# K weights, K products and phi passes divided at column 384 instead of 320

## The chip, the cores and the metric

The kernel runs on one core of one Trainium2 chip. The metric is the device time of one execution in microseconds (us), the median over several runs. The trace beside it is of one profiled execution of the same program; its times are counted from the start of its span. The engines are TensorE (PE in the profile, with its weight loads on a row of their own, PEld), VectorE (DVE), ScalarE (ACT), GpSimd (POOL) and SyncE (SP), which issues most of the DMAs.

## The reference, cut to what matters

Two blocks read the same x (one batch, S = 2048 rows, D = 640 columns), and their results are added to it: linear attention with 32 heads of 20 columns on the layer-normed x, and a small mixture-of-experts style block on the 8 rows with the highest score r.

```python
def _A_ref(x, wqkv, wo):
    qkv = (x @ wqkv).reshape(B, S, 3, H, Dh).transpose(2, 0, 3, 1, 4)
    q, k, v = qkv[0], qkv[1], qkv[2]
    phi = lambda t: jnp.where(t > 0, t + 1, jnp.exp(t)) + 1e-6
    pq, pk = phi(q), phi(k)
    kv = jnp.einsum("bhsd,bhse->bhde", pk, v)
    z = jnp.einsum("bhsd->bhd", pk)
    num = jnp.einsum("bhqd,bhde->bhqe", pq, kv)
    den = jnp.einsum("bhqd,bhd->bhq", pq, z)[..., None] + 1e-6
    return (num / den).transpose(0, 2, 1, 3).reshape(B, S, D) @ wo

def _B_ref(x, w_r, w_gate, w_up, w_down):
    r = x @ w_r
    idx = jnp.argsort(-r, axis=-1)[:, :8]
    x_sel = jnp.take_along_axis(x, idx_e, axis=1)
    y = (silu(x_sel @ w_gate) * (x_sel @ w_up)) @ w_down
    y = y * sigmoid(r at idx)
    return x + y scattered to the rows idx

x = A_x
xn = _layernorm(x)
return x + _A_ref(xn, A_wqkv, A_wo) + _B_ref(xn, B_w_r, B_w_gate, B_w_up, B_w_down)
```

The change touches the K part of `x @ wqkv`, `phi(k)`, and the score `r`, whose weights ride as one more column beside the K weights.

## The kernel before

The 2048 rows are T = 16 tiles of 128 rows. Everything is in bf16 with fp32 sums in PSUM, one tensor `PS` of 8 banks of 512 columns. The order of every engine's work is written out by hand: the calls in the source, from top to bottom, are the order on each engine's queue, and an engine that waits holds up all that stands behind it on that queue.

**First stage, by tile t.** DVE takes the statistics of a tile in two halves of 320 columns (`ln_a`, `ln_b`, lines 151 and 154; these halves stay), aggregates them (`ln_g`), ACT makes 1/sigma of it (`ln_r`, lines 160 and 161), and DVE writes the normed tile into `XX[:, t, 0]` (`ln_xn`, line 165). The transposed tile goes into `xnT`: for t < 4 by PE transposes (`tr_mm`, line 174) and copies out of PSUM (`tr_cp`, lines 181 and 183), from t = 4 on by a DMA transpose on SP's queue (`tr_dma`, line 186). Then `K(t)` (line 210) multiplies with the K weights, which lie in `wk` in two parts: `wkh[0]`, columns 0 to 319 of K, and `wkh[1]`, columns 320 to 639 with the weights of r as a 321st column behind them (written by ACT at line 135). Part h = 0 goes to PSUM bank b, part h = 1 to bank b + 1 (b is 6, for tile 1 it is 4), five matmuls each (KC = 5 row blocks of the weights). Part 1 is placed at column `off(t, 1)` = 15 - t, so that the r column of each tile stays behind in a column of bank 7 of its own; tile 1, in bank 5, is kept separately. From t = 5 on, one weight load of zeros (`pad`, line 249) goes ahead of each part, and two more stand between the matmuls of `G`.

ACT then makes Exp and Relu of each part (`PHe` line 226, `PHr` line 229, both parts in turn by `PHa`), into `ek` and `rk`, 640 columns wide, and DVE joins both parts at once in `PHb` (line 245: min(exp, 1) + relu) into `pk[:, t]`. `G(t)` (lines 254 and 261) sums the product of the normed tile and `pk` over all tiles in banks 0 to 5.

The first four tiles are interleaved by hand in small steps (`KA` is weight blocks 0 and 1, `KB` blocks 2 to 4). From t = 4 on one loop runs: PE has `K(t)` and then `G(t - 1)`; ACT has `PHa(t)`, the small `ln_r(t + 3)`, and for t > 12 a pass `xpx` (line 198, x + xn of one tile); DVE has `PHb(t - 1)`, `ln_xn(t + 2)` and statistics.

**Between the stages.** `corner` (line 275) adds the last block of G in bank 6. `rcopy` (lines 237 and 238) copies the scores out of bank 7, the last of them on DVE; after it `q_pe(0, 0, 7)` (line 482), the first group of the Q products, writes that bank. Then come `PHb(15)` and `G(15)`.

**The rest** (Q products and their phi, denominators, routing and the expert block, the merged output matrix, the output products at line 754) uses none of what is changed, except that `Mb` takes over the place of `wk` later on, at its own width. Its output pieces are also 320 wide, or 256 and 384 for the first four tiles.

**DMA issues at the start.** ACT's queue has the weights of r and then `wkh[0]`; SP's queue has x tiles 0 to 3, one each, then `wkh[1]`, then x in three loads of four tiles.

Of the kernel before, what the change touches and what calls it, by code (L numbers as in the profile page):

```python
# [7 lines left out]
P = 128  # L8
S = 2048
D = 640  # L10
# [3 lines left out]
T = S // P  # L14
KC = D // P
# [14 lines left out]
BF16 = mybir.dt.bfloat16  # L30
# [3 lines left out]
AF = mybir.ActivationFunctionType  # L34
# [4 lines left out]
def kernel(  # L39
# [13 lines left out]
    pe, dve, act, pool, sp = nc.tensor, nc.vector, nc.scalar, nc.gpsimd, nc.sync  # L53
# [3 lines left out]
    wqkv_v = A_wqkv.rearrange("(kc p) n -> p kc n", p=P)  # L57
# [7 lines left out]
    PS = psp.tile([P, 8, 512], F32, name="PS")  # L65

    def st(shape, dt, name, tag=None):
        return sb.tile(shape, dt, name=name, tag=tag or name)
# [5 lines left out]
    wk = st([P, KC, WS], BF16, "wk", "wkM")  # L74
# [16 lines left out]
    rbf = st([P, T], BF16, "rbf")  # L91
# [4 lines left out]
    MR = st([P, T], F32, "MR")  # L96

    HW = 320
    wkh = [wk[:, :, 0:HW], wk[:, :, HW + 64 :]]


    def ld(eng, dst, src):
        eng.dma_start(dst, src)
# [4 lines left out]
    dve.memset(MVf[:], 0.0)  # L108
    wr = st([KC, P], BF16, "wr")
    ld(act, wr[:], B_w_r.rearrange("(kc p) -> kc p", p=P))  # L110
    ld(act, wkh[0], wqkv_v[:, :, D : D + HW])
    ld(sp, XX[:, 1, 1, :], x_v[:, 1, :])
    ld(sp, XX[:, 2, 1, :], x_v[:, 2, :])
    ld(sp, XX[:, 3, 1, :], x_v[:, 3, :])
    ld(sp, wkh[1][:, :, 0:HW], wqkv_v[:, :, D + HW : 2 * D])
    for a, b in ((4, 8), (8, 12), (12, 16)):
        ld(sp, XX[:, a:b, 1, :], x_v[:, a:b, :])
    sp.dma_start_transpose(xnT[:, 0:4, S - P : S], zero[:])
# [1 line left out]
    def warm4(w):  # L120
        pe.matmul(PS[:, 7, 0:w], lhsT=nc.const_aps.tensor(0.0, (P, P), F32),
                  rhs=nc.const_aps.tensor(0.0, (P, w), F32), start=True, stop=True)
# [9 lines left out]
    warm4(256)  # L132
    pe.transpose(PS[:, 3, :].bitcast(BF16)[:, 0:KC], wr[:], ident[0:KC, 0:KC])
    warm4(512)
    act.copy(wkh[1][:, :, HW], PS[:, 3, :].bitcast(BF16)[:, 0:KC])
    kv1 = st([P, NG, GC], BF16, "kv1")
    kv2 = st([P, NG, GC], BF16, "kv2")
    xsT = st([P, KC, 32], BF16, "xsT")
# [62 lines left out]
    def off(t, h):  # L201
        return T - 1 - t if t != 1 and h else 0

    def K(t, hs=(0, 1), b=6, ks=range(KC)):
        for h in hs:
            if t > 4:
                pad(1)
            w = HW + h
            for kc in ks:
                pe.matmul(  # L210
                    PS[:, b + h, off(t, h) : off(t, h) + w],
                    lhsT=xnT[:, kc, t * P : (t + 1) * P],
                    rhs=wkh[h][:, kc, 0:w],
                    start=(kc == 0),
                    stop=(kc == KC - 1),
                )

    phis = {}

    def phi_src(t, h, b):  # L220
        return PS[:, b + h, off(t, h) : off(t, h) + HW]

    def PHe(t, h, b=6):
        if t not in phis:
            phis[t] = tuple(tmp.tile([P, D], BF16, tag=k, name=k, bufs=3) for k in ("ek", "rk"))
        act.activation(phis[t][0][:, h * HW : (h + 1) * HW], phi_src(t, h, b), AF.Exp)  # L226

    def PHr(t, h, b=6):
        act.activation(phis[t][1][:, h * HW : (h + 1) * HW], phi_src(t, h, b), AF.Relu)  # L229

    def PHa(t, hs=(0, 1), b=6):
        for h in hs:
            PHe(t, h, b)
            PHr(t, h, b)

    def rcopy():
        act.copy(rbf[:, 0 : T - 2], PS[:, 7, HW : HW + T - 2])
        dve.tensor_copy(rbf[:, T - 1 : T], PS[:, 7, HW + T - 1 : HW + T])

    def rcopy1(b):  # L240
        act.copy(rbf[:, T - 2 : T - 1], PS[:, b, HW : HW + 1])

    def PHb(t):
        ek, rk = phis[t]
# [2 lines left out]
    def pad(n):  # L247
        for _ in range(n):
            pe.ldweights(zero[:, 0:P])  # L249
# [106 lines left out]
    tr_mm(1, 0, 2)  # L356
    tr_cp(0, 1, 0, act)
    K(0, (0,), 6, KA)
    ln_b(2)
    tr_cp(1, 0, 2, act)  # L360
    tr_mm(1, 1, 2)
    ones(1)
    K(0, (0,), 6, KB)
    tr_cp(1, 1, 2, act)
    ln_g(2)
    ln_a(3)
    K(1, (0,), 4, KA)
    ln_r(2)
    ln_b(3)
    K(1, (0,), 4, KB)  # L370
    PHe(0, 0, 6)
    ln_xn(2)
    K(0, (1,), 6, KA)
    PHr(0, 0, 6)
    K(1, (1,), 4, KA)
    ln_g(3)
# [6 lines left out]
    ln_xn(3)  # L383
    K(1, (1,), 4, KB)
    PHe(0, 1, 6)
    tr_cp(2, 1, 0, dve)
    PHr(0, 1, 6)
    tr_mm(3, 0, 2)
    ln_a(4)
    K(2, (0,), 6, KA)  # L390
    rcopy1(5)
    PHe(1, 0, 4)
    tr_mm(3, 1, 2)
# [100 lines left out]
    for t in range(T - 1):  # L494
        corner(t)
    rcopy()
    q_pe(0, 0, 7)
    PHb(T - 1)
# [457 lines left out]
```

## Time and profile before

| | us |
|---|---|
| median of 3 runs | 106.52 (106.29 to 106.86) |
| the profiled execution's own time | 106.34 |
| its span | 104.6 |
| PE busy in it | 99.7 (95%), granted clock 1.0 throughout |
| DVE busy | 82.8 (79%) |
| ACT busy | 68.8 (66%) |
| the K products, line 210: matmuls | 160 |
| the phi passes, lines 226 and 229: busy | 14.1 and 14.0 |

In the profile's groups of instructions, a row is line, engine, operation, tile written and tiles read, shape, count, then busy time and the mean duration in ns of one. A matmul's duration is its latency, ends are modelled, and matmuls overlap: the rate is read from the chain of waits, where a row is start, time, and the instructions on the chain. In the timeline a row is start, time, engine, line, operation, and in brackets the idle time ahead of it with what ended it; several in a row of one kind are one row, which then shows the shape of the first.

### The profile page before, as it was taken

The page shows a single profiled execution, that of the slowest core. Times are in us where ns is not written, and L with a number is a line of the kernel's source. Part 1 is how long each engine was busy: PE and PEld are TensorE (multiplying, and loading weights), DVE is VectorE, ACT ScalarE, POOL GpSimd, SP SyncE. Part 2 cuts the span into 40 slices and gives each one's busy share as a digit, 9 for nine tenths or more (in the row PEclk, how much of TensorE's full clock was granted, in tenths as well). Part 3 has the DMA queues.
Part 4 walks back from the last instruction along what each step waited for, and adds up shares of the span by engine and source line. Part 5 has one row for each costly group of instructions (what it writes and reads, how often), then busy time and mean ns, then how long its engine had stood idle before and what let it go on. Part 6 is the DMA issues. An engine that isn't in the chain of part 4 may idle for free.

```text
span 104.6 us, 2773 instructions
## 1 busy us (share of the span) xinstructions
PE 99.7 (95%) x916; PEld 72.6 (69%) x1148; DVE 82.8 (79%) x187; ACT 68.8 (66%) x171; POOL 15.9 (15%) x60
## 2 busy tenths in 40 slices
PE   6889999999999999999999999999999999999980
PEld 3257666668888888888777777875567767777760
DVE  1797999988888897873787867878988997888870
ACT  4289957666666666888599999876993996000000
POOL 7800000520000000000000026370000500000140
PEclk9999999999999999999999999999999999999999
DMA  2999938334655555899998999911470136895344
GB/s 67 304 341 382 271 64 58 77 66 96 147 126 101 133 121 117 180 288 337 229 386 282 337 337 379 350 50 39 133 255 9 30 101 205 150 376 211 132 129 125
DMA packets 23024, 19.67 MB, mean 188 GB/s; under 512 B 10594, under 2 KB 21474, under 8 KB 23010
## 3 DMA queue, kind: packets, MB, share of 16 engines
q1 hardware_dynamic: 21880, 19.01, 63.2%
q10 hardware_dynamic: 842, 0.46, 1.6%
q8 instruction: 8, 0.13, 0.5%
q0 software_dynamic: 288, 0.01, 0.3%
q14 instruction: 6, 0.05, 0.1%
HBM read 13.80 MB, written 3.65 MB: 167 GB/s over the span
## 4 chain that ended last, share of the span: by engine, by line
PE 90%; DVE 3%; DMA 2%; issue 1%; DVEq 0%
PE PS L210 21%; PE PS L482 21%; PE PS L754 20%; PE PS L254 15%; PE PS L261 4%; DMA XX<-in_A_x_dram 2%; PE PS L706 2%; PE PS L666 1%; PE PS L548 1%; PE PS L174 1%; PE PS L730 1%; PE PS L677 1%; PE PS L275 1%; DVE stats L151 1%; DVE XX L165 1%
## 5 line engine op out<-in xcount | busy, mean ns | idle before, releaser
L210 PE MATMUL PS<-wk,xnT 128*128 128x320 bf16 (+1 forms) x160 | 25.4, 300 | 0.0
L254 PE MATMUL PS<-pk,XX 128*128 128x512 bf16 x75 | 22.7, 379 | 0.0
L482 PE MATMUL PS<-xnT,wq 128*128 128x512 bf16 x97 | 22.2, 379 | 0.2
L754 PE MATMUL PS<-Mb,pqT 128*128 128x320 bf16 (+4 forms) x165 | 22.1, 295 | 0.0
L249 PEld LDWEIGHTS <-zero 128*128 128x128 bf16 x224 | 18.2, 97 | 5.5
L226 ACT ACTIVATE ek<-PS 128x320 bf16<-128x320 f32 x32 | 14.1, 441 | 9.9 <-PE PS L210 9.9
L754 PEld LDWEIGHTS <-pqT 128*128 128x128 bf16 x165 | 15.8, 98 | 4.7 <-issue 0.3
L210 PEld LDWEIGHTS <-xnT 128*128 128x128 bf16 x160 | 15.2, 97 | 4.7 <-issue 0.2
L245 DVE SCALAR_TENSOR_TENSOR pk<-ek,rk 128x640 bf16<-128x640 bf16 x16 | 13.1, 819 | 4.8 <-ACT rk L229 4.5
L539 DVE SCALAR_TENSOR_TENSOR pqT<-qe,qr 128x512 bf16<-128x512 bf16 x20 | 13.5, 685 | 2.9 <-ACT qr L491 2.9
L490 ACT ACTIVATE qe<-PS 128x512 bf16<-128x512 f32 x20 | 12.3, 616 | 3.2 <-PE PS L482 3.2
L261 PE MATMUL PS<-pk,XX 128*128 128x128 bf16 x64 | 14.0, 219 | 0.3
L229 ACT ACTIVATE rk<-PS 128x320 bf16<-128x320 f32 x32 | 14.0, 438 | 0.0
L482 PEld LDWEIGHTS <-wq 128*128 128x128 bf16 x100 | 11.6, 118 | 2.9 <-issue 0.2
L491 ACT ACTIVATE qr<-PS 128x512 bf16<-128x512 f32 x20 | 12.3, 616 | 0.0
L763 DVE TENSOR_TENSOR o<-PS,XX 128x640 bf16<-128x640 f32 x11 | 9.0, 822 | 2.9 <-PE PS L754 2.0
L254 PEld LDWEIGHTS <-XX 128*128 128x128 bf16 x80 | 7.8, 98 | 4.5
L198 ACT ACTIVATE XX<-XX,MR,SR 128x640 bf16<-128x640 bf16 x11 | 9.4, 913 | 0.0
L151 DVE BATCH_NORM_STATS2 stats<-XX 128x6 f32<-128x320 bf16 x16 | 7.4, 461 | 1.9 <-DMA XX<-in_A_x_dram 1.9
L165 DVE TENSOR_SCALAR XX<-XX,MVf,SR 128x640 bf16<-128x640 bf16 (+2 forms) x17 | 7.2, 432 | 0.6 <-ACT SR L161 0.6
L154 DVE BATCH_NORM_STATS2 stats<-XX 128x6 f32<-128x320 bf16 x16 | 7.7, 480 | 0.0
L267 POOL MEMSET XX<- 128x1 bf16 x18 | 1.8, 102 | 35.7 <-DVE XX L165 20.2
(114 smaller groups left out, 100.0 us busy)
## 6 DMA issues: line engine op xcount, KB each, us to landing
out_dram<-o SPq DMA_DIRECT2D x15, 160.0 KB, 2.0
XX<-in_A_x_dram SPq DMA_DIRECT2D x3, 640.0 KB, 7.9
wg<-in_B_w_gate_dram SPq DMA_DIRECT2D x5, 384.0 KB, 8.6
wu<-in_B_w_up_dram SPq DMA_DIRECT2D x5, 384.0 KB, 6.1
wd<-in_B_w_down_dram SPq DMA_DIRECT2D x1, 1920.0 KB, 10.6
wv<-in_A_wqkv_dram SPq DMA_DIRECT2D x5, 160.0 KB, 3.1
wq<-in_A_wqkv_dram SPq DMA_DIRECT2D x1, 800.0 KB, 5.9
hi_d<-XX SPq DMA_DIRECT2D x1, 800.0 KB, 4.0
```

The costliest lines, as they stand in the source:

```text
L210: pe.matmul(PS[:, b + h, off(t, h) : off(t, h) + w], lhsT=xnT[:, kc, t * P : (t + 1) * P], rhs=wkh[h][:, kc, 0:w], start=(kc == 0), stop=( ...
L226: act.activation(phis[t][0][:, h * HW : (h + 1) * HW], phi_src(t, h, b), AF.Exp)
L229: act.activation(phis[t][1][:, h * HW : (h + 1) * HW], phi_src(t, h, b), AF.Relu)
L245: dve.scalar_tensor_tensor(out=pk[:, t, :], in0=ek[:], scalar=1.0, in1=rk[:], op0=ALU.min, op1=ALU.add)
L249: pe.ldweights(zero[:, 0:P])
L254: pe.matmul(PS[:, a, :], lhsT=lhsT, rhs=pk[:, t, 0:512], start=(t == 0), stop=(t == T - 1),)
L261: pe.matmul(PS[:, 5, a * P : (a + 1) * P], lhsT=lhsT, rhs=pk[:, t, 512:D], start=(t == 0 and a == 0), stop=(t == T - 1), skip_group_check= ...
L482: pe.matmul(PS[:, bank, :], lhsT=by5(wq[:, kc, :])[:, m, :], rhs=xnT[:, kc, tb * TBLK : (tb + 1) * TBLK], start=(kc == 0), stop=(kc == KC ...
L490: act.activation(e, PS[:, bank, :], AF.Exp)
L491: act.activation(r, PS[:, bank, :], AF.Relu)
L539: dve.scalar_tensor_tensor(out=pqT[:, m, tb * TBLK : (tb + 1) * TBLK], in0=e, scalar=1.0, in1=r, op0=ALU.min, op1=ALU.add,)
L754: pe.matmul(PS[:, b, o : o + c1 - c0], lhsT=pqT[:, kc, t * P : (t + 1) * P], rhs=Mb[:, kc, c0:c1], start=(kc == 0), stop=(kc == KC - 1))
```

## The change

The border between part 0 and part 1 of K moves from column 320 to column 384. Part 0 of the weights then has 384 columns, part 1 has 256 and the column for r, at place 256 of that part. The loads of both parts, the K products, the Exp and Relu passes and the places from which the scores are copied follow. No instruction is added, removed or moved on any engine: 80 matmuls go from 320 to 384 columns and 80 from 321 to 257; 32 ACT passes go from 320 to 384 columns and 32 to 256; the load on ACT's queue goes from 5 x 320 to 5 x 384 elements per partition, the one on SP's queue from 5 x 320 to 5 x 256. `PHb`, `G` and all else keep their shapes. All of `wk` is as wide as before, and part 1 still begins at column 384 of it.

```diff
     HW = 320
-    wkh = [wk[:, :, 0:HW], wk[:, :, HW + 64 :]]
+    KH = ((0, 3 * P), (3 * P, D))
+    W1 = D - 3 * P
+    wkh = [wk[:, :, 0 : 3 * P], wk[:, :, 3 * P :]]
...
-    ld(act, wkh[0], wqkv_v[:, :, D : D + HW])
+    ld(act, wkh[0], wqkv_v[:, :, D : D + KH[0][1]])
...
-    ld(sp, wkh[1][:, :, 0:HW], wqkv_v[:, :, D + HW : 2 * D])
+    ld(sp, wkh[1][:, :, 0:W1], wqkv_v[:, :, D + KH[1][0] : 2 * D])
...
-    act.copy(wkh[1][:, :, HW], PS[:, 3, :].bitcast(BF16)[:, 0:KC])
+    act.copy(wkh[1][:, :, W1], PS[:, 3, :].bitcast(BF16)[:, 0:KC])
...
     def K(t, hs=(0, 1), b=6, ks=range(KC)):
...
-            w = HW + h
+            w = KH[h][1] - KH[h][0] + h
...
     def phi_src(t, h, b):
-        return PS[:, b + h, off(t, h) : off(t, h) + HW]
+        return PS[:, b + h, off(t, h) : off(t, h) + KH[h][1] - KH[h][0]]
...
-        act.activation(phis[t][0][:, h * HW : (h + 1) * HW], phi_src(t, h, b), AF.Exp)
+        act.activation(phis[t][0][:, KH[h][0] : KH[h][1]], phi_src(t, h, b), AF.Exp)
...
-        act.activation(phis[t][1][:, h * HW : (h + 1) * HW], phi_src(t, h, b), AF.Relu)
+        act.activation(phis[t][1][:, KH[h][0] : KH[h][1]], phi_src(t, h, b), AF.Relu)
...
     def rcopy():
-        act.copy(rbf[:, 0 : T - 2], PS[:, 7, HW : HW + T - 2])
-        dve.tensor_copy(rbf[:, T - 1 : T], PS[:, 7, HW + T - 1 : HW + T])
+        act.copy(rbf[:, 0 : T - 2], PS[:, 7, W1 : W1 + T - 2])
+        dve.tensor_copy(rbf[:, T - 1 : T], PS[:, 7, W1 + T - 1 : W1 + T])
...
     def rcopy1(b):
-        act.copy(rbf[:, T - 2 : T - 1], PS[:, b, HW : HW + 1])
+        act.copy(rbf[:, T - 2 : T - 1], PS[:, b, W1 : W1 + 1])
```

## The prediction

> **What bounds the kernel now.** I read the page's chain of waits by engine first, then the chain in order of time, then the places in it where PE is not at its rate.
>
> ```profile
> PE 90%; DVE 3%; DMA 2%; issue 1%; DVEq 0%
> 6.97 1.15 PE PS L210 x8
> 8.12 0.03 issue
> 8.15 0.71 PE PS L210 x4
> ...
> 30.19 1.36 PE PS L210 x10
> ...
> 32.85 1.36 PE PS L210 x10
> 34.22 0.22 PE PS L254
> ...
> 52.12 1.08 PE PS L482 x5
> ...
> 77.12 0.55 PE PS L754 x5
> ```
>
> PE is 90% of the chain that ends last, from about 6 us to the end. In the middle of the first stage ten K products, five of 320 and five of 321 columns, take 1.36 us, 136 ns each, in every tile (30.19, 32.85), and one tile follows the other with nothing between. So a change can only gain where PE still stands still, and that is at the start. Two such places are in reach of the K products:
>
> ```profile
> 1.45 0.41 ACTq L103 DMA_DIRECT2D wk<-in_A_wqkv_dram  x1
> 2.68 0.43 SPq L103 DMA_DIRECT2D wk<-in_A_wqkv_dram  x1
> wk<-in_A_wqkv_dram ACTq DMA_DIRECT2D x1, 400.0 KB, 4.6
> wk<-in_A_wqkv_dram SPq DMA_DIRECT2D x1, 400.0 KB, 5.4
> 7.00 0.48 ACT L181 COPY xnT<-PS 128x384 bf16<-128x384 bf16 x1
> 7.53 0.25 PEld L210 LDWEIGHTS <-xnT 128*128 128x128 bf16 x3 [0.22 <-ACT xnT L181]
> 8.15 0.37 PEld L210 LDWEIGHTS <-xnT 128*128 128x128 bf16 x3 [0.23 <-issue]
> ```
>
> The first two rows are the issues of the two weight parts, the next two their sizes and times to landing, the last three ACT's copy and the idle weight loader. In a stream a load of 97 ns follows the next after 136 ns, so 0.04 us of idle is ordinary. At 7.53 the load of tile 1's next part 0 product waited for ACT's copy of the transposed tile, which ended at 7.48 (0.05 us to hand over); a load runs one product ahead, so 0.22 - 0.04 - 0.136 = 0.05 us of PE is lost. At 8.15 stands the first part 1 product: its weights land at 2.68 + 5.4 = 8.08, and here the product itself waited, so 0.23 - 0.04 = 0.19 us is lost. Both together: 0.24 us that PE could win.
>
> **The change part by part.**
>
> *The products themselves.* 256 columns take 0.55 / 5 = 110 ns (the row at 77.12), 512 take 1.08 / 5 = 216 ns (52.12), so 0.414 ns a column between them: 384 columns 163 ns, 257 columns 110 ns. A tile's ten are 5 x 273 = 1.37 us against 1.36. Over 16 tiles that is at most 16 x 0.007 = 0.11 us by rows rounded to 0.01, and I take nothing, since both splits stream 641 columns. Bounds: 0 and +0.11.
>
> A rule speaks against this. The Trainium skill, "TensorE: Matmul & The Clock Gate", section "LDWEIGHTS (loading the stationary operand)", gives a load of 128 columns 128 / 1.2, an estimate of 107 ns. A 257 column product would still just cover one load, but the padding load and the real one ahead of part 1 would take 214 ns behind a 136 ns product now and behind a 163 ns one after, so 11 tiles would win 11 x 0.027 = 0.30 us. The trace disagrees: there the ten products of a padded tile take the same 136 ns each.
>
> *The wait at 7.53.* It goes: five part 0 products of 27 ns more each come ahead of it, 0.135 us against 0.05.
>
> *The wait for part 1's weights.* Now PE needs them later: ten part 0 products stand ahead, 10 x 0.027 = 0.27, less the 0.05 that the other wait gave, so 0.22 us later, against a loss of 0.19. Its load is 80 KB smaller and shares the DMA engines with part 0's, 80 KB larger, so the sum ahead of its last byte is unchanged. I take it as landing at 8.08 as before; the wait is gone. After it the ten part 1 products of tiles 0 and 1 are 0.27 us shorter. Gain at the end of tile 1: 0.24 us.
>
> *Part 0's weights.* They now hold 480 KB. These rows give the rate while they load and the first use:
>
> ```profile
> 4.00:5.00 1.00, 0.91 (x2) 0.08 (x1) 0.97 (x5) 0.47 (x3) 0.85 (x4) 1.00 1.08 339
> 5.00:6.00 1.00, 0.46 (x5) 0.28 (x5) 1.00 (x4) 0.74 (x4) 0.18 (x1) 1.00 1.00 323
> 6.36 0.30 PE L210 MATMUL PS<-wk,xnT 128*128 128x320 bf16 x1
> ```
>
> They land at 1.45 + 4.6 = 6.05 and are used at 6.36: cover 0.31 us. The last column is GB/s: 80 KB (81,920 bytes) at 323 to 339 are 0.24 to 0.25 us if nothing else moves. So it lands by 6.30, before its use, and costs nothing, with 0.06 to spare. If the whole 4.6 us grew with the bytes, it would be 0.92 later, and 0.61 after its use: that is the upper end.
>
> *ACT's passes.* Nothing but the split of ACT's work changes, and its lag:
>
> ```profile
> L226 ACT ACTIVATE ek<-PS 128x320 bf16<-128x320 f32 x32 | 14.1, 441 | 9.9 <-PE PS L210 9.9
> L490 ACT ACTIVATE qe<-PS 128x512 bf16<-128x512 f32 x20 | 12.3, 616 | 3.2 <-PE PS L482 3.2
> 46.89 0.44 ACT L226 ACTIVATE ek<-PS 128x320 bf16<-128x320 f32 x1 [0.41 <-PE PS L210]
> 47.23 0.43 ACT L229 ACTIVATE rk<-PS 128x320 bf16<-128x320 f32 x1
> 47.58 0.44 ACT L226 ACTIVATE ek<-PS 128x320 bf16<-128x320 f32 x1
> 47.91 0.43 ACT L229 ACTIVATE rk<-PS 128x320 bf16<-128x320 f32 x1
> 48.23 0.92 ACT L198 ACTIVATE XX<-XX,MR,SR 128x640 bf16<-128x640 bf16 x1
> 49.04 0.17 ACT L237 CAST rbf<-PS 128x14 bf16<-128x14 f32 x1
> ```
>
> From 441 to 616 ns over 192 columns is 0.91 ns a column, so a pass of 384 takes 58 ns more than one of 320 and one of 256 takes 58 less; two of each make no sum. But part 0 is complete 5 x 27 = 0.135 us later, and ACT, which waits for it (0.41 idle ahead of 46.89), starts later by that. The four passes ran 46.89 to 48.23, 1.34 us, where two pairs without a gap are about 1.32 (0.33 from start to start), so 0.02 is given back: ACT finishes a tile 0.11 us later relative to PE. Where PE or DVE wait for that, it counts. In the loop:
>
> ```profile
> 20.24 0.44 ACT L226 ACTIVATE ek<-PS 128x320 bf16<-128x320 f32 x1 [0.80 <-PE PS L210]
> 32.39 0.83 DVE L245 SCALAR_TENSOR_TENSOR pk<-ek,rk 128x640 bf16<-128x640 bf16 x1 [0.48 <-ACT rk L229]
> ```
>
> DVE joins the halves of the tile of 30.19 by 33.22 and `G` uses them after the next K products, at 34.22: about 1.0 us of cover, so the lag of 0.11 costs nothing there. Behind `PHb` on DVE stand the next tile's norm and its DMA transpose; they shift by the same 0.11. The tight place is the end of the stage:
>
> ```profile
> 49.24 0.16 DVE L238 CAST rbf<-PS 128x1 bf16<-128x1 f32 x1 [1.59 <-ACT rbf L237]
> 49.52 1.24 PE L482 MATMUL PS<-xnT,wq 128*128 128x512 bf16 x4
> ```
>
> The score copy on DVE ends at 49.40, waiting for ACT's copy, and the Q products that write this bank start at 49.52: 0.12 us, of which about 0.05 is handing over (as from ACT to the weight load, 7.48 to 7.53). The lag of 0.11 exceeds the remaining 0.07: PE waits 0.04 us. Bounds: 0 (if the copies wait for PE alone) and 0.11.
>
> *How much of the 0.24 us gets through.* PE arriving earlier meets what does not move with it.
>
> ```profile
> 9.11 0.45 DVE L165 TENSOR_SCALAR XX<-XX,MVf,SR 128x640 bf16<-128x640 bf16 x1 [0.60 <-ACT SR L161]
> 10.34 0.81 DVE L245 SCALAR_TENSOR_TENSOR pk<-ek,rk 128x640 bf16<-128x640 bf16 x1
> 11.43 0.38 PE L254 MATMUL PS<-pk,XX 128*128 128x512 bf16 x1
> 13.95 0.43 ACT L229 ACTIVATE rk<-PS 128x320 bf16<-128x320 f32 x1
> 14.26 0.29 ACT L160 ACTIVATE lnv<-MVf,eps 128x1 f32<-128x1 bf16 x1
> 14.83 0.45 DVE L165 TENSOR_SCALAR XX<-XX,MVf,SR 128x640 bf16<-128x640 bf16 x1
> 15.30 1.21 SPq L186 DMA_TRANSPOSE xnT<-XX  x1
> 19.19 0.54 PEld L210 LDWEIGHTS <-xnT 128*128 128x128 bf16 x4
> DMA to landing us min/median/max: 2.6/2.6/3.9
> ```
>
> The first `G` needs tile 0's `pk`: DVE, busy without a gap since 9.11, ends it at 11.15; with 0.05 to hand over and about 0.06 for the weight load behind that wait, `G` cannot start before 11.26, so of 0.24 us 0.17 is left. Then tile 5: its transpose is issued at 15.30 behind ACT's `ln_r(5)` (14.26) and DVE's norm (14.83), and this is the one that takes the longest, 3.9 us: it lands at 19.2, as PE's weight load for `K(5)` starts (19.19). That load runs beside a 512 column product, so it may come 0.12 later without harm. ACT's two passes of tile 3's part 0 ahead of `ln_r(5)` start with PE (0.17 earlier, then 0.135 later for the wider part) and are 0.117 longer, so the transpose comes some 0.08 later, against a cover of 0.12: 0.04 to 0.12 of the gain passes. I take 0.12, what remains without the delay, since the idle ACT had there swallows part of it. The transposes of the later tiles land 2.6 us after issue by the median.
>
> *Sum* against the profiled execution: span 104.6 - 0.12 + 0.04 = 104.5; its own time 106.34 - 0.08 = 106.26. The median of the runs is 0.18 above that execution, so the forecast is 106.52 - 0.08, rounded to 106.4. A difference of 0.5% (0.53 us) is about what a measurement of this kernel can tell from none; this is a fifth of it.
>
> **The rivals.**
>
> *Part 0's weights late (not faster, up to 106.9).* Any delay above 0.31 us holds PE from 6.36 on. For: the DMA engines are saturated there (share 1.00 to 1.08). Against: 0.25 us by rate. At the upper end PE loses 0.61, of which the two waits it then no longer has return 0.24: 106.52 + 0.37 + 0.04 = 106.9; worse only if x tiles 2 and 3 are late as well.
>
> *ACT's lag is paid in each tile (slower).* If `G(t)` waited for `PHb(t)`, or `K(t + 1)` for the bank that `PHr` frees, each of the 11 tiles of the steady loop from t = 5 would cost 0.11: 106.52 + 1.2 = 107.7. It decides from the point where the cover at `G` is below 0.11. Against: 1.0 us of it, and 0.41 us (46.89) to 0.80 us (20.24) of ACT's idle time in a tile; for: nothing but that the chain holds no reserve on PE.
>
> *The waits at the start are larger in most runs than in this one (faster).* The profiled execution is 0.18 below the median. If the part 1 weights usually land later by that, and neither the first `G` nor tile 5 holds PE, the gain is 0.24 + 0.18 = 0.42: 106.1; with 0.24 for 80 KB less on its queue, 105.9. Against: the two floors above.
>
> *Exposed weight loads.* The mechanism: two loads in a row that the product ahead does not cover, a gain of 11 x 0.027 = 0.30 from the longer product ahead of part 1, 106.1 with the rest. Against: ten padded products at 136 ns.
>
> **How the numbers follow.** Forecast 0.68, part 0 late 0.12, ACT's lag 0.05, larger waits 0.13, exposed loads 0.02. Slower by over 0.5% (above 107.05): the 0.05 of ACT's lag and 0.04 of the late weights. Faster by over 0.5% (below 105.99): 0.05 of the larger waits and 0.01 for the rest. That leaves 0.85 within. The three runs before scatter by 0.3 to either side; with the bounds of the sum (-0.24 to +0.11 + 0.11) and the two milder rivals the range is 106.0 to 106.9, and what it leaves out holds under 0.2.
>
> **What would show it.** In the profile after: the weight loader's idle rows ahead of 7.5 and 8.15 gone or small; the first part 0 product still at about 6.36 (later: the late load); ten K products in 1.36 to 1.37 us; passes of 499 and 383 ns; the join of a tile on DVE about 0.1 later against PE, without a wait on PE in the loop; the first Q product a few hundredths behind the corner products; `G`'s first product waiting for `pk`, and `K(5)` for its transpose. The prediction is wrong if PE shows a wait in each tile, or if the first K product comes after 6.6.

## The result, and the profile after

The changed kernel takes 106.81 us, the median of 20 runs (106.45 to 107.89); the kernel before, in as many runs beside it, 106.38 us (106.23 to 106.9). The ratio is 1.0033, 95% interval 1.0018 to 1.0049: slower by a third of a percent, where 0.08 us less had been forecast. The time lies within the range of 106.0 to 106.9 that was given, but not on the side that was forecast. The scatter is part of the result: the fastest runs lie 0.2 us apart, the slowest 1.0. Every ratio here is worked out from the single runs of both kernels, without the few in the chip's slower state, while the medians are over all runs, so a ratio need not equal that of the medians.

The profiled execution of the changed kernel took 106.51 us, with a span of 104.8. It is one of its better ones. Its chain of waits (start, time, what) at the places shown of before; line 212 is the K products (210 before), 256 and 263 are G (254 and 261), 176 the transposes, 183 ACT's copies of them, 123 the warm-up products:

```profile
3.86 2.00 PE PS L123 x2
5.86 0.18 PE PS L176 x2
...
6.06 0.38 ACT xnT L183
...
6.49 0.50 PE PS L212 x2
6.99 0.17 PE PS L176 x3
7.16 1.74 PE PS L212 x12
...
30.22 1.36 PE PS L212 x10
...
32.89 1.36 PE PS L212 x10
34.25 0.22 PE PS L256
```

The steady loop is as it was: ten products in 1.36 us, `G` right behind, no wait. The twelve products from 7.16 on follow each other without a stop: both waits that PE could win, at 7.53 and 8.15, are gone. The loss is elsewhere. The weight loader (PEld) and the engines ahead of it, between 8 and 10 us:

```profile
8.01 0.47 ACT L228 ACTIVATE ek<-PS 128x384 bf16<-128x384 f32 x1
8.38 0.48 ACT L231 ACTIVATE rk<-PS 128x384 bf16<-128x384 f32 x1
8.74 0.29 ACT L162 ACTIVATE lnv<-MVf,eps 128x1 f32<-128x1 bf16 x1
9.07 0.20 ACT L163 ACTIVATE SR<-lnv 128x1 f32<-128x1 f32 x1
9.31 0.45 DVE L167 TENSOR_SCALAR XX<-XX,MVf,SR 128x640 bf16<-128x640 bf16 x1 [0.61 <-ACT SR L163]
9.81 0.11 PEld L176 LDWEIGHTS <-XX 128*128 128x128 bf16 x2 [0.26 <-DVE XX L167]
```

This wait is not in the profile of before. Tile 3's transposes need its norm, which DVE makes at 9.31 (9.11 before), behind ACT's `ln_r(3)` at 8.74 (8.54 before), which stands on ACT's queue behind the two passes of tile 0's part 0, now 384 wide, and behind the copies that PE's wider part 0 products let begin later. The loader is idle 0.26 us where 0.01 is ordinary between part 1 products of 257 columns and loads of 98 ns; PE loses about 0.14 us by the starts of its matmuls.

The end of the first stage, DVE's copy of the last score and the first Q product (line 484):

```profile
49.38 0.16 DVE L240 CAST rbf<-PS 128x1 bf16<-128x1 f32 x1 [1.58 <-ACT rbf L239]
...
49.59 1.24 PE L484 MATMUL PS<-xnT,wq 128*128 128x512 bf16 x5
```

The copy ends at 49.54 and the product starts at 49.59; from the first corner product to it are 0.88 us, 0.84 before. And the passes themselves, by the groups of instructions with shapes apart (busy time, mean ns, idle time ahead):

```profile
L228 ACT ACTIVATE ek<-PS 128x384 bf16<-128x384 f32 x16 | 7.9, 493 | 9.6 <-PE PS L212 9.6
L231 ACT ACTIVATE rk<-PS 128x256 bf16<-128x256 f32 x16 | 6.4, 403 | 0.0
L228 ACT ACTIVATE ek<-PS 128x256 bf16<-128x256 f32 x16 | 6.3, 392 | 0.6 <-PE PS L212 0.6
```

This execution is only 0.17 us slower than the profiled one of before, and the medians are 0.43 apart. What the others have, a second profiled execution of the same kernel showed.

### The profile page after: what moved, and what is told of

It reads as the page before. It is cut to its first block, busy times and chain, and to the rows that moved or that the text cites. A ratio compares the mean times of both kernels' runs of the same rounds, so it can differ in the third digit from the quotient of the medians.

```text
span 104.8 us, 2781 instructions
## 1 busy us (share of the span) xinstructions
PE 100.9 (96%) x924; PEld 72.9 (70%) x1148; DVE 82.7 (79%) x187; ACT 68.2 (65%) x171; POOL 16.4 (16%) x60
## 4 chain that ended last, share of the span: by engine, by line
PE 95%; issue 1%; DVE 1%; ACT 0%; DVEq 0%
PE PS L212 21%; PE PS L484 21%; PE PS L756 20%; PE PS L256 16%; PE PS L123 5%; PE PS L263 3%; PE PS L708 2%; PE PS L668 1%; PE PS L550 1%; PE PS L176 1%; PE PS L732 1%; PE PS L679 1%; PE PS L277 1%; DVE o L769 1%; PE PS L630 1%
## 5 line engine op out<-in xcount | busy, mean ns | idle before, releaser
L212 PE MATMUL PS<-wk,xnT 128*128 128x384 bf16 (+1 forms) x160 | 25.2, 300 | 0.1
L256 PE MATMUL PS<-pk,XX 128*128 128x512 bf16 x80 | 23.5, 379 | 0.0
L228 ACT ACTIVATE ek<-PS 128x384 bf16<-128x384 f32 (+1 forms) x32 | 14.2, 443 | 10.1 <-PE PS L212 10.1
L231 ACT ACTIVATE rk<-PS 128x384 bf16<-128x384 f32 (+1 forms) x32 | 14.3, 446 | 0.0
```

Of the source, the lines that this page charges most:

```text
L212: pe.matmul(PS[:, b + h, off(t, h) : off(t, h) + w], lhsT=xnT[:, kc, t * P : (t + 1) * P], rhs=wkh[h][:, kc, 0:w], start=(kc == 0), stop=( ...
L228: act.activation(phis[t][0][:, KH[h][0] : KH[h][1]], phi_src(t, h, b), AF.Exp)
L231: act.activation(phis[t][1][:, KH[h][0] : KH[h][1]], phi_src(t, h, b), AF.Relu)
L256: pe.matmul(PS[:, a, :], lhsT=lhsT, rhs=pk[:, t, 0:512], start=(t == 0), stop=(t == T - 1),)
```

## The experiments

**e1: the changed kernel again.**

> The changed kernel once more, for more executions and a second profile. Theory A (the cost arises at the start: the larger part 0 load delays x tiles 2 and 3 or is itself late, and the wider part 0 products and passes hold up ACT's chain for tiles 3 and 5, so PE waits at tile 3's transposes or at K(5)): 0.3 to 0.5 us slower than before by the median, and the profile shows PE waits between 6 and 20 us. Theory B (ACT's lag is paid at the end of the first stage, where the score copies hold the first Q product): the profile shows a wait of 0.04 us or more at 49.5 and the rest equal to before. Rival C (nothing but scatter): within 0.1 us of before.

Measured: 106.73 us, 12 runs, ratio 1.0031 (1.0008 to 1.0053). Its profiled execution took 107.03 us. The chain at its start, the timeline row of the first product, and the row of the load (KB and us to landing):

```profile
1.45 5.60 DMA wk<-in_A_wqkv_dram
7.05 0.04 issue
7.09 0.49 PE PS L212 x2
...
7.09 0.32 PE L212 MATMUL PS<-wk,xnT 128*128 128x384 bf16 x1 [0.53 <-DMA wk<-in_A_wqkv_dram]
```

```profile
wk<-in_A_wqkv_dram ACTq DMA_DIRECT2D x1, 480.0 KB, 5.6
```

The load of part 0 stands on the chain: it lands 5.6 us after its issue, and the first K product starts at 7.09 instead of 6.36. The wait at tile 3 is there too (the starts of the matmuls show about 0.15 us lost), and so is the one of 0.05 us at the end of the stage.

**e2: only tiles 4 to 15 divided at 384.** To divide tiles apart, K's columns lie side by side in the weight tile, `cut(t)` gives the column, and part 1 of the late tiles is placed 64 columns higher in PSUM.

```diff
-    wkh = [wk[:, :, 0:HW], wk[:, :, HW + 64 :]]
+    LW = 320
+
+    def cut(t):
+        return 320 if t < 4 else 384
...
-        return T - 1 - t if t != 1 and h else 0
+        return T - 1 - t + cut(t) - HW if t != 1 and h else 0
...
-            w = HW + h
+            w = span(t, h)[1] - span(t, h)[0] + h
```

> Loads and tiles 0 to 3 divided at 320 as before, tiles 4 to 15 at 384, with K's columns side by side in the weight tile and part 1 of the late tiles placed 64 columns higher so that the scores stay in the same places. Theory A: no more than 0.1 us slower than before, since loads and the first four tiles are as before. Theory B: the whole difference, 0.3 to 0.5 us slower.

Measured: 106.71 us, ratio 1.0013 (0.9989 to 1.0037) against 106.45. In its profile the first K product is at 6.39, tile 3's transposes wait for nothing, the 0.88 us to the first Q product are there. The time cannot tell the theories apart. The profile puts the wide parts of the late tiles at 0.04 us; it does not show where the rest of the 0.26 us between the medians would come from, if it is real.

**e3: only tiles 0 to 3, and the loads, at 384** (`cut(t)` turned round, loads of 384 and 256).

> Loads and tiles 0 to 3 divided at 384 as in the change, tiles 4 to 15 at 320. Theory A: 0.3 to 0.5 us slower than before, with more scatter. Theory B: within 0.1 us of before or faster by up to 0.24.

Measured: 106.60 us, ratio 1.0005 (0.9984 to 1.0027). Theory A expected 0.3 to 0.5 us; this is a miss. The interval reaches up to 0.3 us, into the interval of the change. In the profile the first load landed after 4.7 us, the first product started at 6.50, and nothing waited at the end of the stage: 0.84 us. Tile 3's transposes waited here too, and PE lost about 0.21 us there.

**e4: only the loads at 384 and 256**, products and passes at 320, with K's columns side by side in the weight tile as in e2.

```diff
+    LW = 384
...
-    ld(act, wkh[0], wqkv_v[:, :, D : D + HW])
+    ld(act, wk[:, :, 0:LW], wqkv_v[:, :, D : D + LW])
...
-    ld(sp, wkh[1][:, :, 0:HW], wqkv_v[:, :, D + HW : 2 * D])
+    ld(sp, wk[:, :, LW:D], wqkv_v[:, :, D + LW : 2 * D])
```

> Only the two weight loads are divided at 384; all products and passes at 320 as before. If the larger load on ACT's queue is the cause (it delays x tiles 2 and 3, or lands late itself): 0.3 us or more slower than before, with more scatter. If the wider products and passes ahead of ACT's small steps are the cause: within 0.1 us of before.

Measured: 106.82 us, ratio 1.0042 (1.0013 to 1.007): the loads alone make a difference as large as the whole change, though e3, with the same loads, did not show it. Its profile begins like e1's:

```profile
1.45 5.50 DMA wk<-in_A_wqkv_dram
6.94 0.04 issue
6.99 0.43 PE PS L219 x2
```

**e5: the same with 448 and 192 columns** (`LW = 448`).

> As e4 (products and passes all at 320), but the first load takes 448 columns and the second 192: the suspected cost doubled. In e1 and e4 the first K product waited 0.7 us for the first load, which landed at 6.9 to 7.1 instead of 6.0 in the profile of before. Theory A (the larger first load lands late): the landing moves on to 7.0 or later in the profile and the median is 0.5 us or more above before. Rival (it is the landing's own scatter, whatever the size): as e4 or nearer to before, with a landing anywhere between 6 and 7.

Measured: 107.05 us against 106.61 beside it, ratio 1.0027 (1.0001 to 1.0053); 0.44 us is a little under the 0.5 expected, and the times do not tell e5 from e4. The landing moved on:

```profile
wk<-in_A_wqkv_dram ACTq DMA_DIRECT2D x1, 560.0 KB, 6.0
```

```profile
7.50 0.43 PE L219 MATMUL PS<-wk,xnT 128*128 128x320 bf16 x2 [0.92 <-DMA wk<-in_A_wqkv_dram]
```

**e8: the changed kernel with ACT's score copy ahead of the last x + xn pass of the loop.**

```diff
-        if t > 12:
+        if 12 < t < T - 1:
             xpx(t - 13)
...
     rcopy()
+    xpx(2)
     q_pe(0, 0, 7)
```

> The changed kernel with ACT's copy of the scores ahead of the last x + xn pass of the loop instead of behind it. Theory B (part of the cost is the 0.04 to 0.05 us wait of the first Q product at 49.5): that wait is gone in the profile, and the median falls by about 0.05 us, which the rounds can hardly tell; the rest of the cost stays. If the score copies are the larger part: the median falls by 0.2 us or more.

Measured: 106.82 us against 106.61, ratio 1.0015 (0.9988 to 1.0043). The wait is gone, 0.84 us from the first corner product (line 277) to the first Q product:

```profile
49.33 1.00 PE L277 MATMUL PS<-pk,XX 128*128 128x128 bf16 x15
50.16 0.38 PE L484 MATMUL PS<-xnT,wq 128*128 128x512 bf16 x1
```

So that wait is worth 0.04 us. This execution, too, took its first K product late, at 7.12, its load landing after 5.6 us.

**e6 and e7: each weight load cut in two by row blocks**, in the changed kernel and in the one before.

```diff
-    ld(act, wkh[0], wqkv_v[:, :, D : D + KH[0][1]])
+    for k0, k1 in ((0, 2), (2, KC)):
+        ld(act, wkh[0][:, k0:k1], wqkv_v[:, k0:k1, D : D + KH[0][1]])
...
-    ld(sp, wkh[1][:, :, 0:W1], wqkv_v[:, :, D + KH[1][0] : 2 * D])
+    for k0, k1 in ((0, 2), (2, KC)):
+        ld(sp, wkh[1][:, k0:k1, 0:W1], wqkv_v[:, k0:k1, D + KH[1][0] : 2 * D])
```

> The changed kernel with each of the two weight loads cut in two by row blocks: blocks 0 and 1 first, then 2 to 4, which the first products use in that order. Theory A: the wait of the first K product goes, since a first piece of 192 KB lands well before 6.3, and the time falls by 0.3 us or more against the changed kernel, to the time of before or below it; 0.05 remains for the score copies. Rival (the loads are not the cause): stays 0.3 us above before.

> The kernel before with its two weight loads cut in the same way. Theory A: also faster than before, by 0.1 to 0.25 us, since the waits at 6.36 (in executions where the first load is late) and at 8.15 go; e6 and e7 then differ by about 0.05. Rival: no difference from before.

Measured: 107.45 us (7 runs), ratio 1.0086 (1.0054 to 1.0117), and 106.94 us, 1.0057 (1.0024 to 1.009). Both slower, a plain miss. In e6 the second piece of the first load landed only at 7.13 and held the products behind it, 0.15 us of PE. Yet e7's profile has the first K product at 6.34, the first part 1 product at 7.93 (8.15 before), and the last weight load of the program at 101.27 (101.46 before). The loss is behind that: 3.52 us to the end of the span instead of 3.16. At the end SP works off the DMA semaphores one by one, always in the same order, about 0.06 us each. Two more DMAs shift the semaphores, so that the last landing counted on the first of that list and not on the last of it: from the last landing to the end there are 1.31 us in e6 and e7, 0.93 in all the others. That is the loss of the two profiled executions, which were the fastest of their runs. The other runs went up to 107.80 and 108.04, and what they lost beyond it, no profile shows.

**e11 and e12: the same with the number of DMAs kept**, two loads of the gate and two of the up weights being joined for it.

```diff
-            for k in range(KC):
+            for k in range(KC - 2):
                 ld(sp, wg[:, k, :], wg_v[:, k, :])
+            ld(sp, wg[:, KC - 2 : KC, :], wg_v[:, KC - 2 : KC, :])
```

> e7 again, with the same number of DMAs as before: the last two row blocks of the gate weights are one load, and so are those of the up weights. e7's profile had every product of the output 0.19 us earlier than before and yet a longer span, because its last DMA's semaphore came first in the list that SP works off at the end: 1.31 us from the last landing to the end against 0.94. Theory A: that comes back, 0.94 us, and the median is 0.1 to 0.3 us below before. Rival (splitting costs in itself): still 0.3 us above before.

> The same for the changed kernel. Theory A: without the late first load the change costs only what tile 3's transposes and the score copies cost, so 0.1 to 0.3 us above e11 and within 0.15 us of before. If the cost of the change lies elsewhere: 0.3 us or more above before and e11 alike.

Measured: 106.56 us, ratio 1.0016 (0.9993 to 1.0038), and 106.74 us, 1.0026 (0.9998 to 1.0055), against 106.45. The time from the last landing to the end is back at 0.93 us in both. e11's execution took 106.26 us, but its median is no better than that of before; e12 is 0.18 above e11, as expected, and 0.29 above before, which is more than expected. Neither is shown to beat the kernel before. e12's profile has next to no wait for the load (0.02 us, for its second piece), but one for tile 3's norm (0.13 us), 0.88 us at the end of the stage, and a wait for something that the change does not touch, at the first output product, whose denominators go through DRAM:

```profile
76.59 0.83 DVE L579 TENSOR_TENSOR pqT<-pqT,R 128x1280 bf16<-128x1280 bf16 x1 [0.74 <-DMA R<-rd_d]
```

That wait comes and goes in both kernels: in five profiled executions each, the same row had 0 to 0.70 us of idle time ahead of it before, and 0.32 to 0.81 in the changed kernel.

**e9, e10, e15, e16: the kernel before, and e13, e14: the changed one, one profiled execution each.**

> The kernel before, looked at again, to see how its first weight load lands in other executions. Theory A (a smaller load lands early enough): between 5.9 and 6.5 us, and the first K product waits 0.2 us or less. Rival (the landing scatters between 6 and 7 whatever the size): a landing near 7 and a wait of 0.5 us or more is as likely as in the changed kernel.

> One more look at the kernel before, with the expectations of e9: theory A a landing of the first load between 5.9 and 6.5 us and a wait of 0.2 us or less; the rival a landing near 7 us in about every second look.

> The kernel before once more. Theory A: a landing of the first load at 6.5 us or earlier, and a first K product at 6.5 or earlier, as in its three looks so far. Rival: a landing near 7 and a first product at 6.9 or later.

> The kernel before once more, with the expectations of e15: theory A a first K product at 6.5 us or earlier; the rival at 6.9 or later, in one of these two looks at least.

> Another look at the changed kernel. Theory A (its larger first load lands late in about every second execution): a first K product at 6.5 us or at about 7.1, and from there to the last product of G(14) 41.8 us in either case. Rival (the late landing of the other looks was scatter that the kernel before shares): the first K product at 6.4 to 6.5 in this look and the next.

> The changed kernel once more, with the expectations of e13: theory A a first K product at 6.5 us or at about 7.1; the rival at 6.4 to 6.5 in both looks.

Their times were 106.33, 106.73, 106.26 and 106.50 us, and 107.88 and 106.85. The profiled executions with whole loads together, times in us:

| kernel, execution | KB in the first load | to landing | first K product | to the first corner product | on to the first Q product |
|---|---|---|---|---|---|
| before | 400 | 4.6 | 6.36 | 42.32 | 0.84 |
| before, e9 | 400 | 4.7 | 6.39 | 42.15 | 0.84 |
| before, e10 | 400 | 5.0 | 6.46 | 42.21 | 0.84 |
| before, e15 | 400 | 4.5 | 6.41 | 42.17 | 0.84 |
| before, e16 | 400 | 4.5 | 6.35 | 42.47 | 0.84 |
| late tiles only, e2 | 400 | 4.9 | 6.39 | 42.42 | 0.88 |
| changed | 480 | 4.5 | 6.49 | 42.23 | 0.88 |
| changed, e1 | 480 | 5.6 | 7.09 | 42.21 | 0.88 |
| changed, e8 | 480 | 5.6 | 7.12 | 42.21 | 0.84 (copy moved) |
| changed, e13 | 480 | 5.3 | 6.83 | 42.53 | 1.50 |
| changed, e14 | 480 | 5.0 | 6.46 | 42.21 | 0.88 |
| loads only, e4 | 480 | 5.5 | 6.99 | 42.14 | 0.84 |
| tiles 0 to 3, e3 | 480 | 4.7 | 6.50 | 42.28 | 0.84 |
| e5 | 560 | 6.0 | 7.50 | 42.15 | 0.84 |

The 400 KB load never took more than 5.0 us in six executions, the 480 KB one 5.3 to 5.6 in four of seven. At the kernel before, no landing near 7 came up, as theory A expected; e13's 6.83 lies between the two values that theory A named, and the rival, 6.4 to 6.5 in both e13 and e14, fell with it. In the changed kernel's executions but the first, the first product starts 0.04 us behind the landing, so the load is what releases it (in e13 the profile names ACT's copy, which ended within 0.01 us of the landing). At the kernel before that is so in e10 alone (and in e2, whose load has 400 KB too); in the other four the product starts 0.3 to 0.5 us behind.

The first product stands at 6.39 by the mean of the five executions of before and at 6.80 by that of the changed kernel's five: 0.40 us. The way from there to the corner products is equal by the mean, 42.26 and 42.28. The two long ones, 42.47 and 42.53, are one of each kernel; in both, x's tile 2 landed late, and DVE's statistics waited for it until 6.47 (e16) and 7.00 (e13). From the first Q product to the end of the span there are 55.1 to 55.5 us before and 55.1 to 55.6 in the changed kernel. The 1.50 of e13 is a late load of the Q weights, as its chain shows. This load is the same in both kernels, and whether the change has a part in its lateness is not shown:

```profile
43.63 7.18 DMA wq<-in_A_wqkv_dram
50.81 0.05 issue
50.85 0.41 PE PS L484
```

## Why the prediction was wrong, step by step

**The products.** Right. 384 and 257 columns take together what 320 and 321 take; ten in 1.36 us. The exposed weight loads of the fourth rival do not show, before or after.

**The step that failed: "it lands by 6.30, before its use, and costs nothing, with 0.06 to spare".** The load of 480 KB was given a cover of 0.31 us and, at a mean rate, a price of 0.25 us. The cover holds by the mean of the five executions of before, 0.28 us, though it ranges from nothing (e10) to 0.46. The price was wrong: 80 KB more moved the landing by 0.54 us by the mean (4.66 to 5.20 over the five executions of each kernel), and in the bad ones by about a microsecond. The first product came 0.40 us later by the mean, and after 6.6, the prediction's own sign of being wrong, in three of five. A load is complete when the slowest of its 16 parts has landed: by the trace's record of each landing, the parts came from 4.47 to 6.00 us in the profile of before, and in e8 fifteen of them by 6.03 and the last at 7.07. The Trainium skill says this in "DMA: Bandwidth & Descriptors", section "Why a DMA increments its semaphore by 16 and not by 1": only the full count of 16 means that all data has landed. The trace agrees. The mean rate over all engines says nothing of such a last part. The rival "part 0's weights late" named this, with its mechanism and up to 0.4 us, but was given 0.12. Its condition for worse came up as well: x's tile 3, issued behind these loads, landed 4.2 to 4.7 us after its issue in before and 4.5 to 5.2 in the changed kernel.

**The wait for part 1's weights: mis-sized.** It was booked as 0.19 us won in each execution. In the five executions of before it is there twice (0.19, and 0.16 in e16), and three times not at all: 0.07 us by the mean. The profiled execution that the prediction was built on was one of the two, which is bad luck.

**How much gets through: wrong place.** The first `G` and tile 5's transpose were named as what PE would meet when early. The first thing it met was tile 3's transposes, at 9.8, because ACT's chain of small steps runs behind the wide passes of tile 0: 0.13 to 0.15 us of wait in the changed kernel's first profile, in e1 and e14, and in e8 and e12; e13, with x's tile 2 late, lost more. The prediction saw the same lag 5 us later, for tile 5 (14.83 to 15.10 us in the profile after), where it cost nothing. Nor was the 0.24 us there to be won in most executions. Where before has no wait for part 1's weights, PE already reaches tile 3's transposes about when they come ready, as in e10, where the starts of the matmuls show 0.06 us lost:

```profile
9.76 0.11 PEld L174 LDWEIGHTS <-XX 128*128 128x128 bf16 x2 [0.22 <-DVE XX L165]
```

What the wider part 0 wins on PE it gives back there, and nothing was left of the gain: 42.26 against 42.28.

**The score copies.** Right in place and size: 0.04 us forecast, 0.04 measured, and gone when ACT copies first (e8).

**ACT's passes and the loop.** Right: 493 and 392 ns for Exp where 499 and 383 were worked out, and no wait of PE in the loop; that rival fell.

**The sum as it came out**, from the table: 0.40 at the first product, 0.02 to the corner products, 0.04 to the first Q product (e8 and e13 left out), 0.46 us by the means of the profiled executions; the medians of 20 runs differ by 0.43. e13's 0.62 us for the Q weights is not in it.

What is shown is where the profiled executions lose time: at the landing of the first load, which by the mean comes later the larger the load. e4 shows loads of these sizes slower by themselves. What is not settled is how much of the timed difference this explains. e3, with the same loads, is 0.15 us above before where 0.3 to 0.5 was expected. e12, with next to no wait for the load, is still 0.29 above, so taking the late load away did not bring the time back. e2 and e11 lie 0.26 and 0.11 above too, and none of the four is clear of before; with intervals of 0.2 to 0.3% the timed runs do not fix the shares. Nor do the runs tell the bytes of the first load from the length of its rows (640, 768 and 896 bytes), which grew with it while the rows of the other load shrank. Why single parts of the first load come a microsecond late was not tried.

## What to carry to other kernels

The cover of a load must be taken from several executions, not from the gap in one profile: its price is that of its slowest part, and here, with the DMA engines busy throughout, a fifth more bytes moved the landing by about twice what the mean rate says. Time won on an engine that is busy throughout is only kept if everything that feeds it moves too, so the next thing that is due must be looked for right behind the place of the gain, on the small steps of other engines. And a change that leaves the order and the sum of the work alone still moves the first use of what is loaded.

## What was not expected of the hardware

The end of the program depends on which semaphore the last DMA counts on: SP reads the list in a fixed order at about 0.06 us each. With the last landing on the first entry 1.31 us pass to the end of the span (e6 and e7), with it on the last entry 0.93 us (all the others). Two more DMAs at the start of the program cost 0.37 us at its end in these profiles.
